# A decode-attention kernel with ScalarE's steady state as a loop, TensorE's loop two tiles longer, and the first output projection in two column tiles

## Chip, cores, metric

The kernel runs on one core of one Trainium2 chip. The metric is device time of one execution, in microseconds (us); lower is better. Engines are named as in the profile: PE is TensorE's matmuls and PEld its weight loads, DVE is VectorE, ACT is ScalarE, POOL is GpSimd, and SP is SyncE, which here only issues DMA. A name with "q" at its end (SPq) is that engine's sequencer.

## The reference

Two independent attention blocks A and B, each with batch 8, one query position, 32 heads of 128, and a cache of 4096 positions, all in bf16; their results are concatenated.

```python
q = (x @ wq).reshape(B, 1, 32, 128).transpose(0, 2, 1, 3)      # x: [8, 1, 1024]
scores = einsum("bhqd,bhkd->bhqk", q, k_cache) * 128 ** -0.5   # k_cache: [8, 32, 4096, 128]
p = softmax(scores)
o = einsum("bhqk,bhkd->bhqd", p, v_cache)
out = o.transpose(0, 2, 1, 3).reshape(B, 1, 4096) @ wo
```

Every element of the caches is read once, so the kernel has to bring 1107 MB into SBUF.

## The kernel before

The work is cut into 64 tiles (`NQ`), one for each block, group of eight heads, and batch. A tile is 8 MB of K and 8 MB of V. Three SBUF slots (`ring`) hold K and V tiles in turn. The order on the DMA queue is wq A, K0, wq B, K1, V0, K2, V1, K3, and so on. SP issues the load of a tile when the last reader of the slot's previous tenant has finished.

```python
plan = [("wq", 0, 1), ("k", 0, 0), ("wq", 1, 2)]          # kind, number, slot
for n in range(NQ - 1):
    plan.append(("k", n + 1, (n + 1) % 2))
    plan.append(("v", n, 2))                              # every V but the last goes to slot 2
```

For each K tile, DVE multiplies by the broadcast query and folds once, in four chunks (`NR = 4`); PE sums the rest; DVE finishes the scores; ACT takes the exponential; PE multiplies with V. The query vectors come from two projections. Each is transposed by PE into PSUM (`misc`), and DVE copies it to SBUF (`qT`). The second projection and its four copies stand inside tile 0:

```python
def make_qT(c):
    for hb in range(HB):
        ...                                               # PE transposes eight heads into misc
        opQT[c] = opQT["last"] = add("dve", lambda e, hb=hb: e.tensor_copy(
            qT[:, c, hb * HQ * B:(hb + 1) * HQ * B], misc_bf16[:, 0:HQ * B]), [op])   # contiguous

for n in range(NQ):
    for r in range(NR):
        make_mul(s); make_red(s - 1); ...; fold = make_fold(s)
        if n == 0 and r == 1:
            make_q(1); make_qT(1)                         # waits for wq B
        if r == 2 and n >= 1: make_pv(n - 1, 0, RG // 2)
        if r == 3 and n >= 1: make_pv(n - 1, RG // 2, RG); make_acc(n - 1)
        if r == 2 and n + 1 < NQ: make_stage(n + 1); make_qbc(n + 1)
        make_eacc(s, fold); load_tiles(); ...
```

PE and DVE run tiles 3 to 62 as a loop of two tiles each; ACT's code is written out for all 64 tiles. At the end come the two output projections, each 128 matmuls of 256 columns in four column tiles of the array. The last weights arrive in three pieces, of 24, 6 and 2 rows (`wo_cuts`).

Of the kernel before, what the change touches and what calls it, by code (L numbers as in the profile page):

```python
# [13 lines left out]
class _Op:  # L14
    __slots__ = ("eng", "emit", "deps", "dma_key", "token", "sig")

    def __init__(self, eng, emit, deps, dma_key=None):
        self.eng = eng
        self.emit = emit
        self.deps = [d for d in deps if d is not None]  # L20
        self.dma_key = dma_key
        self.token = None
        self.sig = False
# [7 lines left out]
class _Program:  # L31
# [11 lines left out]
    def add(self, eng, emit, deps=(), dma_key=None):  # L43
        op = _Op(eng, emit, list(deps), dma_key)
        if dma_key is not None:
            self.counts[dma_key] = self.counts.get(dma_key, 0) + 16
            op.token = (dma_key, self.counts[dma_key])
        for d in op.deps:
            if not (d.eng == "pe" and eng == "pe"):
                d.sig = True  # L50
        self.ops[eng].append(op)
        return op
# [13 lines left out]
    def _waits(self, engname):  # L66
        waited, out = {}, []
        for op in self.ops[engname]:
            need = {}
            for d in op.deps:  # L70
                if d.eng == "pe" and engname == "pe":
                    continue
                key, val = d.token
                if need.get(key, 0) < val:
                    need[key] = val
            left = []
            for key, val in need.items():
                if waited.get(key, 0) < val:
                    waited[key] = val
                    left.append((key, val))  # L80
            out.append(left)
        return out

    def run(self, engname, eng, sems, loop=None):
        ops, waits = self.ops[engname], self._waits(engname)

        def emit(op):
            ins = op.emit(eng)
            if op.dma_key is not None:
                ins.then_inc(sems[op.dma_key], 16)  # L90
            elif op.sig:
                ins.then_inc(sems[op.eng], 1)

        def straight(lo, hi):
            for op, left in zip(ops[lo:hi], waits[lo:hi]):
                for key, val in left:
                    eng.wait_ge(sems[key], val)
                emit(op)
# [8 lines left out]
        step = {}  # L107
        for j in range(size):
            rows = [waits[lo + j] for lo in at[:-1]]
            for i, row in enumerate(rows):  # L110
                assert [k for k, _ in row] == [k for k, _ in rows[0]], (engname, j, i, rows[0], row)
                assert ops[at[i] + j].sig == ops[at[0] + j].sig
                for (key, val), (_, base) in zip(row, rows[0]):
                    if i:
                        assert (val - base) % i == 0 and step.setdefault(key, (val - base) // i) * i == val - base, (engname, j, key)
        straight(0, at[0])
        with eng.Fori(0, rounds) as i:
            grown = {s: eng.snap(i * s) for s in sorted(set(step.values()))}
            for j in range(size):
                for key, val in waits[at[0] + j]:  # L120
                    eng.wait_ge(sems[key], grown[step[key]] + val)  # L121
                emit(ops[at[0] + j])
        straight(at[-1], len(ops))


LOOPS = {"pe": True, "dve": True}


def _build_kernel(nc, caches, out):
# [21 lines left out]
    with es:  # L151
# [22 lines left out]
        o_sb = sb("o_sb", [128, NC, B * H], FP32)  # L174
        rl = sb("rl", [128, B], FP32)
        on_sb = sb("on_sb", [128, NC, H, B], BF16)
        orow = sb("orow", [128, DT], BF16)
# [44 lines left out]
        opOc, opNorm, opProj, opUse, opPM = {}, {}, {}, {}, {}  # L222
# [15 lines left out]

        def tile_of(kind, n):
            return ring[:, slot[(kind, n)], :]  # L240

        def load_tiles():
            while issued[0] < len(plan):
# [6 lines left out]
                if kind in ("k", "v"):  # L250
                    blk, b = divmod(n, B)
                    c, hb = divmod(blk, HB)
# [28 lines left out]
        def make_qT(c):  # L281
            for hb in range(HB):
                rows = slice(32 * hb, 32 * hb + B)

                def emit(e, rows=rows):
# [6 lines left out]
                    qT[:, c, hb * HQ * B:(hb + 1) * HQ * B], misc_bf16[:, 0:HQ * B]), [op])  # L292

        def make_stage(n):
            blk, b = divmod(n, B)
            c, hb = divmod(blk, HB)
            from_ = qT[:, c, :].rearrange("p (h b) -> p h b", b=B)[:, hb * HQ:(hb + 1) * HQ, b]
            opSt[n] = add("act", lambda e: e.activation(qst[:, n % 2, :].rearrange("p (j m) -> p j m", m=MP),  # L298
                                                        from_.unsqueeze(2).to_broadcast([128, HQ, MP]), ACTF.Copy),
                          [opQT[c], _at(opQb, n - 2)])  # L300
# [22 lines left out]
        def make_eacc(s, fold):  # L323
# [9 lines left out]
            opEacc[s] = add("pe", emit, [fold, c_ident, _at(opRed, s - 2)])  # L333
# [10 lines left out]
        def make_shift(n):  # L344
# [6 lines left out]
            opExp[n] = add("act", lambda e: e.activation(pe[:], s_sb[:, n % 2, :], ACTF.Exp, bias=ngm[:, n % 2:n % 2 + 1], scale=scale,  # L351
                                                         accum_out=rsum[:, n:n + 1]),
                           [opNgm[n], _at(opPM, n - 1)])
# [24 lines left out]
        def make_ext(n):  # L378
            blk, b = divmod(n, B)
            c, hb = divmod(blk, HB)  # L380
# [10 lines left out]
            opOc[n] = add("act", lambda e: e.activation(o_sb[MB * hb:MB * (hb + 1), c, H * b:H * (b + 1)], to, ACTF.Copy), [opExt[n]])  # L391


        def make_norm(c):
            ns = range(c * HB * B, (c + 1) * HB * B)

            def emit(e):
                for hb in range(HB):
                    x = e.matmul(misc[MB * hb:MB * (hb + 1), 0:B], own_m[:].rearrange("p j u -> p (j u)"),
                                 rsum[:, (c * HB + hb) * B:(c * HB + hb + 1) * B], start=True, stop=True, tile_position=(0, MB * hb))  # L400
# [4 lines left out]
                on_sb[:, c].rearrange("p r b -> p b r"), o_sb[:, c, :].rearrange("p (b r) -> p b r", b=B),  # L405
                rl[:].unsqueeze(2).to_broadcast([128, B, H]), ALU.mult), [rec, opOc[ns[-1]]])

        def make_proj(c):
            w = tile_of("wo", c)
            for i, (r0, r1) in enumerate(wo_cuts if c == NC - 1 else ((0, H),)):  # L410
                def emit(e, r0=r0, r1=r1):
                    for r in range(r0, r1):
                        for q in range(NT):
                            col = r * D + q * DT
                            x = e.matmul(proj[32 * q:32 * q + B, 0:DT], on_sb[:, c, r, :], w[:, col:col + DT],  # L415
                                         start=(r == 0), stop=(r == H - 1), tile_position=(0, 32 * q))
                    return x
                opProj[c] = add("pe", emit, [opNorm[c], opT[("wo", c, i)], c_proj] + outs[:1])
            ev = add("dve", lambda e: e.tensor_copy(orow[0:96 + B, :], proj[0:96 + B, 0:DT]), [opProj[c]] + outs[1:])  # L419
            outs[:] = [ev]  # L420
            outs.extend(dma(out[:, 0, c * D + q * DT:c * D + (q + 1) * DT], orow[32 * q:32 * q + B, :], ("out", 0), [ev],
                            "sp" if q % 2 == 0 else "act") for q in range(NT))
# [67 lines left out]
        loop = (3, 2, (NQ - 4) // 2)  # L490
# [6 lines left out]
        @block.tensor  # L497
        def _(eng):
            P.run("pe", eng, sems, loop if LOOPS["pe"] else None)

        @block.scalar
        def _(eng):
            P.run("act", eng, sems)

        @block.vector
        def _(eng):
            P.run("dve", eng, sems, loop if LOOPS["dve"] else None)
# [39 lines left out]
```

## Time and profile before

| | before |
|---|---|
| time, median of 3 runs | 2566.49 us (2566.16 to 2568.4) |
| span of the profiled run | 2565.5 us |
| DMA engines | 99.8% of 16 engines' span, mean 432 GB/s |
| busy: DVE, PE, ACT | 85%, 43%, 5% |

From the page of the kernel before: the DMA row of the 40 slices of the span (9 means 90% or more busy), GB/s in the same slices, and the queues (packets, MB, share of 16 engines).

```profile
DMA  9999999999999999999999999999999999999998
GB/s 425 426 437 431 435 431 435 431 436 431 435 435 432 435 431 436 430 437 430 437 431 435 431 434 432 434 433 433 433 433 432 434 433 433 433 434 432 434 432 379
...
q1 hardware_dynamic: 19360, 1107.32, 99.8%
q8 instruction: 9, 0.15, 0.0%
q10 hardware_dynamic: 96, 0.05, 0.0%
q14 instruction: 5, 0.04, 0.0%
```

There is no slack in the DMA engines. Each packet of 64 KB takes 2.42 us in nearly every case, so an engine runs at a pace of its own, and a tile of 8 MB lands every 19.35 us. The two "instruction" queues, 0.19 MB here, are the engines' program code.

The end, in the chain of waits of the kernel before (start, duration, what):

```profile
2521.07 36.21 DMA ring<-in_B_wo_dram
2557.29 0.14 issue
2557.43 5.35 PE proj L415 x117
2562.78 0.02 issue
2562.80 0.42 DVE orow L419
```

The first piece of the last weights lands at 2557.29 us, the projection takes 5.35 us, the copy 0.42 us, and the output's DMA carries the span to 2565.5 us.

### The profile page before, as it was taken

Reading aid. Unit: us, or ns where it says so; the run is one execution under the profiler, and the core shown is the slowest. Engines: PE = TensorE matmul, PEld = TensorE weight load, DVE = VectorE, ACT = ScalarE, POOL = GpSimd, SP = SyncE. Lnnn points to the kernel's source line nnn. Section 1 sums busy time; section 2 is a strip of 40 time slices with the busy share of each in tenths; the row PEclk is TensorE's granted clock in tenths of the full one; section 3 lists DMA queues with packets and bytes.
Section 4 is the critical chain, followed back from the end, with each engine's and each line's share of the span. In section 5 each row is a group of like instructions: output and inputs, shape, how many; then the busy total and the mean of one; then the engine's idle time right before and its main releaser. Section 6 shows DMA issues by size and latency. Waiting matters only on the chain.

```text
span 2565.5 us, 18370 instructions
## 1 busy us (share of the span) xinstructions
PE 1106.8 (43%) x7712; PEld 393.2 (15%) x7712; DVE 2170.7 (85%) x1043; ACT 129.9 (5%) x401; POOL 2.5 (0%) x14
## 2 busy tenths in 40 slices
PE   2543443443444444444443434444434434434434
PEld 0111111111111111111111111111111111111112
DVE  2898898898898898898888888988988988988983
ACT  1100000000000000000000000000000000000000
POOL 0000000000000000000000000000000000000000
PEclk7676676766766766766767767667766767667667
DMA  9999999999999999999999999999999999999998
GB/s 425 426 437 431 435 431 435 431 436 431 435 435 432 435 431 436 430 437 430 437 431 435 431 434 432 434 433 433 433 433 432 434 433 433 433 434 432 434 432 379
DMA packets 19470, 1107.56 MB, mean 432 GB/s; under 512 B 2224, under 2 KB 2288, under 8 KB 2432
## 3 DMA queue, kind: packets, MB, share of 16 engines
q1 hardware_dynamic: 19360, 1107.32, 99.8%
q8 instruction: 9, 0.15, 0.0%
q10 hardware_dynamic: 96, 0.05, 0.0%
q14 instruction: 5, 0.04, 0.0%
HBM read 1107.33 MB, written 0.03 MB: 432 GB/s over the span
## 4 chain that ended last, share of the span: by engine, by line
DMA 51%; DVE 28%; issue 16%; PE 4%; another core or an unknown queue 0%; ACT 0%; DVEq 0%; SPq 0%
DMA ring<-in_B_k_cache_dram 25%; DMA ring<-in_A_k_cache_dram 25%; DVE ring L316 10%; DVE ring L321 10%; PE red L331 4%; DVE s_sb L339 4%; DVE PM L356 3%; DMA ring<-in_B_wo_dram 1%; DVE rmax L345 1%; DVE rtmp L346 0%; PE proj L415 0%; ACT PM L277 0%; PE o L271 0%; DVEq L121 0%
## 5 line engine op out<-in xcount | busy, mean ns | idle before, releaser
L316 DVE TENSOR_TENSOR ring<-ring,qbc 128x8192 bf16<-128x8192 bf16 x256 | 1132.0, 4422 | 305.5 <-DMA ring<-in_B_k_cache_dram 153.9
L331 PE MATMUL red<-ring,ident 128*128 128x512 bf16 x2048 | 775.6, 548 | 1396.5 <-DVE ring L321 1396.5
L321 DVE TENSOR_TENSOR ring<-ring 128x4096 bf16<-128x4096 bf16 x256 | 582.6, 2276 | 0.0
L331 PEld LDWEIGHTS red<-ring,ident 128*128 128x128 bf16 x2048 | 237.7, 127 | 1843.6 <-DVE ring L321 1498.7
L339 DVE TENSOR_REDUCE s_sb<-red 128x64 f32<-128x1024 f32 x256 | 312.2, 1220 | 2.5 <-PE red L331 2.5
L368 PE MATMUL pv<-ring,PM 128*32 128x512 bf16 x4096 | 269.5, 410 | 4.6 <-DVE PM L356 4.6
L356 DVE TENSOR_TENSOR PM<-pe,own_h 128x2048 bf16<-128x2048 bf16 x64 | 146.2, 2285 | 0.7 <-ACT pe L351 0.7
L368 PEld LDWEIGHTS pv<-ring,PM 128*32 128x32 bf16 x4096 | 103.2, 103 | 182.8 <-issue 108.0
L305 ACT ACTIVATE qbc<-misc 128x128 bf16<-128x128 f32 x64 | 17.7, 277 | 1070.0 <-PE misc L303 1070.0
L351 ACT ACTIVATE pe<-s_sb,ngm 128x256 bf16<-128x256 f32 x64 | 32.5, 508 | 477.3 <-DVE ngm L349 477.3
L376 ACT ACTIVATE accS<-pv 128x512 bf16<-128x512 f32 x64 | 38.2, 597 | 356.3 <-PE pv L368 356.3
L386 PEld LDWEIGHTS o<-accS,E 128*32 128x32 bf16 x1024 | 31.4, 101 | 49.8 <-issue 48.6
L386 PE MATMUL o<-accS,E 128*32 128x32 bf16 x1024 | 38.1, 185 | 0.7 <-ACT accS L376 0.7
L391 ACT ACTIVATE o_sb<-o 32x32 f32<-32x32 f32 x64 | 11.8, 185 | 440.5 <-PE o L386 439.8
L291 DVE COPY qT<-misc 128x64 bf16<-128x64 bf16 x8 | 1.5, 192 | 33.1 <-PE misc L287 33.1
L345 DVE TENSOR_REDUCE rmax<-s_sb 128x1 f32<-128x256 f32 x64 | 26.9, 420 | 2.2
L419 DVE CAST orow<-proj 104x256 bf16<-104x256 f32 x2 | 0.8, 425 | 27.6 <-PE proj L415 27.6
L415 PE MATMUL proj<-ring,on_sb 128*8 128x256 bf16 x256 | 11.1, 357 | 18.5 <-DMA ring<-in_A_wo_dram 9.6
L298 ACT ACTIVATE qst<-qT 128x128 bf16<-128x128 bf16 x64 | 18.7, 293 | 1.0 <-DVE qT L291 1.0
L346 DVE TENSOR_SCALAR rtmp<-half,rmax 128x32 f32<-128x32 f32 x64 | 15.5, 242 | 2.2
L271 PE MATMUL o<-ring,xT 128*8 128x512 bf16 x64 | 7.0, 615 | 20.0 <-DMA ring<-in_A_wq_dram 11.0
L349 DVE TRANSPOSE_TENSOR_REDUCE ngm<-rtmp 128x1 f32<-128x32 f32 x64 | 13.5, 211 | 2.2
(33 smaller groups left out, 74.9 us busy)
## 6 DMA issues: line engine op xcount, KB each, us to landing
ring<-in_B_wo_dram SPq DMA_DIRECT2D x1, 6144.0 KB, 36.2
ring<-in_B_wo_dram SPq DMA_DIRECT2D x1, 1536.0 KB, 39.5
ring<-in_A_k_cache_dram SPq DMA_DIRECT2D x32, 40.0
ring<-in_A_v_cache_dram SPq DMA_DIRECT2D x32, 27.9
ring<-in_B_k_cache_dram SPq DMA_DIRECT2D x32, 39.8
ring<-in_B_v_cache_dram SPq DMA_DIRECT2D x32, 27.9
ring<-in_B_wo_dram SPq DMA_DIRECT2D x1, 512.0 KB, 40.3
out_dram<-orow SPq DMA_DIRECT2D x4, 4.0 KB
```

The costliest lines, as they stand in the source:

```text
L298: opSt[n] = add("act", lambda e: e.activation(qst[:, n % 2, :].rearrange("p (j m) -> p j m", m=MP), from_.unsqueeze(2).to_broadcast([128, ...
L305: opQbc[n] = add("act", lambda e: e.activation(qbc[:, n % 2, :], misc[:, 0:Dh], ACTF.Copy), [opQb[n], _at(opMul, NR * (n - 2) + NR - 1)])
L316: opMul[s] = add("dve", lambda e: e.tensor_tensor(v, v, qbc[:, n % 2, :].unsqueeze(1).to_broadcast([128, CT, Dh]), ALU.mult), [opT[("k", n ...
L321: return add("dve", lambda e: e.tensor_tensor(v[:, :, 0:64], v[:, :, 0:64], v[:, :, 64:128], ALU.add), [opMul[s]])
L331: i = e.matmul(dst, ident[:], v[:, g, :, j, :], start=(j == 0), stop=(j == 3))
L339: opRed[s] = add("dve", lambda e: e.tensor_reduce(s_sb[:, n % 2, r * CT:(r + 1) * CT], red_ps[s % 2][:, :].rearrange("p (t w) -> p t w", w ...
L345: m = add("dve", lambda e: e.tensor_reduce(rmax[:], s_sb[:, n % 2, :], AX.X, ALU.max), [opRed[NR * n + NR - 1]])
L351: opExp[n] = add("act", lambda e: e.activation(pe[:], s_sb[:, n % 2, :], ACTF.Exp, bias=ngm[:, n % 2:n % 2 + 1], scale=scale, accum_out=rs ...
L356: opPM[n] = add("dve", lambda e: e.tensor_tensor(PM[:], pe[:].unsqueeze(2).to_broadcast([128, T, HQ]), own_h[:].unsqueeze(1).to_broadcast( ...
L368: i = e.matmul(pv_ps[32 * q:32 * (q + 1), :], PM[:, t:t + 4, :].rearrange("p t j -> p (t j)"), v[:, t * Dh:(t + 4) * Dh], start=(g == 0), ...
L376: opAcc[n] = add("act", lambda e: e.activation(accS[:], pv_ps[:], ACTF.Copy), [opPV[n], _at(opExt, n - 1)])
L386: x = e.matmul(to, E[:, i, PH - 1 - u:PH - 1 - u + MB], accS[:, i * 128 + H * u:i * 128 + H * (u + 1)], start=(i == 0 and u == 0), stop=(i ...
```

## The change

The intent is to make the program shorter: ACT's 60 steady tiles become a loop of four tiles, PE's loop starts at tile 1 instead of 3, and the first output projection becomes 64 matmuls of 512 columns. The program builds ACT's loop on addresses that move by a constant each round, so tiles are now visited with batch outside the head group, `o_sb` is flattened, and `qT` is stored batch by batch. The core of the diff (the bookkeeping of waits against loop counters is cut):

```diff
-                    blk, b = divmod(n, B)
-                    c, hb = divmod(blk, HB)
+                    c, b, hb = where(n)              # n // (B * HB), n // HB % B, n % HB
...
                 opQT[c] = opQT["last"] = add("dve", lambda e, hb=hb: e.tensor_copy(
-                    qT[:, c, hb * HQ * B:(hb + 1) * HQ * B], misc_bf16[:, 0:HQ * B]), [op])
+                    qT[:, c].rearrange("p (b h) -> p h b", h=H)[:, hb * HQ:(hb + 1) * HQ, :],
+                    misc_bf16[:, 0:HQ * B].rearrange("p (j b) -> p j b", b=B)), [op])
...
-        from_ = qT[:, c, :].rearrange("p (h b) -> p h b", b=B)[:, hb * HQ:(hb + 1) * HQ, b]
+            def emit(e, at):
+                from_ = qT[:].rearrange("p c n -> p (c n)")[:, bass.ds(at(n * HQ, HQ), HQ)]
...
-            opEacc[s] = add("pe", emit, [fold, c_ident, _at(opRed, s - 2)])
+            opEacc[s] = add("pe", emit, [fold, c_E, _at(opRed, s - 2)])
...
+            nt = NT if c == NC - 1 else NT // 2
+            dt = D // nt
...
-        loop = (3, 2, (NQ - 4) // 2)
+        loops = {"pe": (1, 2, (NQ - 2) // 2), "dve": (3, 2, (NQ - 4) // 2), "act": (3, HB, (NQ - 4) // HB)}
```

More of the change, by code (lines that the diff above doesn't have):

```diff
@@ L14, with __init__ @@
 class _Op:
-    __slots__ = ("eng", "emit", "deps", "dma_key", "token", "sig")
-    def __init__(self, eng, emit, deps, dma_key=None):
+    __slots__ = ("eng", "emit", "deps", "dma_key", "token", "sig", "moves")
+    def __init__(self, eng, emit, deps, dma_key=None, moves=False):
         self.eng = eng
         self.emit = emit
+        self.moves = moves
         self.deps = [d for d in deps if d is not None]
@@ L41, in __init__, with add @@
         self.marks = {}
-    def add(self, eng, emit, deps=(), dma_key=None):
-        op = _Op(eng, emit, list(deps), dma_key)
+    def add(self, eng, emit, deps=(), dma_key=None, moves=False):
+        op = _Op(eng, emit, list(deps), dma_key, moves)
         if dma_key is not None:
@@ L66, in _waits @@
     def _waits(self, engname):
-        waited, out = {}, []
+        waited, out, known = {}, [], []
         for op in self.ops[engname]:
@@ L75, in _waits, with emit @@
                     need[key] = val
-            left = []
+            left = {}
             for key, val in need.items():
                 if waited.get(key, 0) < val:
-                    waited[key] = val
-                    left.append((key, val))
+                    left[key] = val
             out.append(left)
-        return out
+            known.append(dict(waited))
+            waited.update(left)
+        return out, known
     def run(self, engname, eng, sems, loop=None):
-        ops, waits = self.ops[engname], self._waits(engname)
-        def emit(op):
-            ins = op.emit(eng)
+        ops = self.ops[engname]
+        waits, known = self._waits(engname)
+        def emit(op, at=lambda base, step: base):
+            ins = op.emit(eng, at) if op.moves else op.emit(eng)
             if op.dma_key is not None:
@@ L95, in straight @@
             for op, left in zip(ops[lo:hi], waits[lo:hi]):
-                for key, val in left:
+                for key, val in left.items():
                     eng.wait_ge(sems[key], val)
@@ L106, in run, with place @@
         assert all(y - x == size for x, y in zip(at, at[1:]))
-        step = {}
+        body, step = [], {}
         for j in range(size):
             rows = [waits[lo + j] for lo in at[:-1]]
-            for i, row in enumerate(rows):
-                assert [k for k, _ in row] == [k for k, _ in rows[0]], (engname, j, i, rows[0], row)
+            row = {}
+            for key in rows[1]:
+                grow = rows[2][key] - rows[1][key]
+                row[key] = rows[1][key] - grow
+                assert step.setdefault(key, grow) == grow
+                assert rows[0].get(key) == row[key] or key not in rows[0] and row[key] <= known[at[0] + j].get(key, 0), (engname, j, key)
+            for i, r in enumerate(rows):
                 assert ops[at[i] + j].sig == ops[at[0] + j].sig
-                for (key, val), (_, base) in zip(row, rows[0]):
-                    if i:
-                        assert (val - base) % i == 0 and step.setdefault(key, (val - base) // i) * i == val - base, (engname, j, key)
+                assert set(r) <= set(row) and (i == 0 or r == {key: val + i * step[key] for key, val in row.items()}), (engname, j, i)
+            body.append(row)
         straight(0, at[0])
         with eng.Fori(0, rounds) as i:
-            grown = {s: eng.snap(i * s) for s in sorted(set(step.values()))}
+            grown = {x: eng.snap(i * x) for x in sorted(set(step.values()))}
+            moved = {}
+            def place(base, x):
+                if x not in moved:
+                    moved[x] = eng.snap(i * (x * per))
+                return moved[x] + base
             for j in range(size):
-                for key, val in waits[at[0] + j]:
+                for key, val in body[j].items():
                     eng.wait_ge(sems[key], grown[step[key]] + val)
-                emit(ops[at[0] + j])
+                emit(ops[at[0] + j], place)
         straight(at[-1], len(ops))
-LOOPS = {"pe": True, "dve": True}
 def _build_kernel(nc, caches, out):
@@ L173, in _build_kernel @@
         accS = sb("accS", [128, 512], BF16)
-        o_sb = sb("o_sb", [128, NC, B * H], FP32)
+        o_sb = sb("o_sb", [128, NC * B * H], FP32)
         rl = sb("rl", [128, B], FP32)
         on_sb = sb("on_sb", [128, NC, H, B], BF16)
-        orow = sb("orow", [128, DT], BF16)
+        orow = sb("orow", [128, 2 * DT], BF16)
         q_sb = PM[:].rearrange("p t j -> p (t j)").rearrange("p (c n) -> p c n", c=NC)
@@ L221, in _build_kernel @@
         opPV, opAcc, opExt, opSt, opQb, opQbc, opQ, opQs, opQT = {}, {}, {}, {}, {}, {}, {}, {}, {}
-        opOc, opNorm, opProj, opUse, opPM = {}, {}, {}, {}, {}
+        opOc, opNorm, opProj, opUse, opPM, opEv = {}, {}, {}, {}, {}, {}
         outs = []
@@ L237, in _build_kernel, with where @@
         issued = [0]
+        def where(n):
+            return n // (B * HB), n // HB % B, n % HB
         def tile_of(kind, n):
@@ L291, in make_qT @@
                 opQT[c] = opQT["last"] = add("dve", lambda e, hb=hb: e.tensor_copy(
-                    qT[:, c, hb * HQ * B:(hb + 1) * HQ * B], misc_bf16[:, 0:HQ * B]), [op])
+                    qT[:, c].rearrange("p (b h) -> p h b", h=H)[:, hb * HQ:(hb + 1) * HQ, :],
+                    misc_bf16[:, 0:HQ * B].rearrange("p (j b) -> p j b", b=B)), [op])
         def make_stage(n):
-            blk, b = divmod(n, B)
-            c, hb = divmod(blk, HB)
-            from_ = qT[:, c, :].rearrange("p (h b) -> p h b", b=B)[:, hb * HQ:(hb + 1) * HQ, b]
-            opSt[n] = add("act", lambda e: e.activation(qst[:, n % 2, :].rearrange("p (j m) -> p j m", m=MP),
-                                                        from_.unsqueeze(2).to_broadcast([128, HQ, MP]), ACTF.Copy),
-                          [opQT[c], _at(opQb, n - 2)])
+            def emit(e, at):
+                from_ = qT[:].rearrange("p c n -> p (c n)")[:, bass.ds(at(n * HQ, HQ), HQ)]
+                return e.activation(qst[:, n % 2, :].rearrange("p (j m) -> p j m", m=MP),
+                                    from_.unsqueeze(2).to_broadcast([128, HQ, MP]), ACTF.Copy)
+            opSt[n] = add("act", emit, [opQT[n // (B * HB)], _at(opQb, n - 2)], moves=True)
         def make_qbc(n):
@@ L350, in make_shift @@
                                                             apply_transpose=True), [t, _at(opExp, n - 2)])
-            opExp[n] = add("act", lambda e: e.activation(pe[:], s_sb[:, n % 2, :], ACTF.Exp, bias=ngm[:, n % 2:n % 2 + 1], scale=scale,
-                                                         accum_out=rsum[:, n:n + 1]),
-                           [opNgm[n], _at(opPM, n - 1)])
+            opExp[n] = add("act", lambda e, at: e.activation(pe[:], s_sb[:, n % 2, :], ACTF.Exp, bias=ngm[:, n % 2:n % 2 + 1], scale=scale,
+                                                             accum_out=rsum[:, bass.ds(at(n, 1), 1)]),
+                           [opNgm[n], _at(opPM, n - 1)], moves=True)
         def make_pm(n):
@@ L378, in make_ext @@
         def make_ext(n):
-            blk, b = divmod(n, B)
-            c, hb = divmod(blk, HB)
+            hb = where(n)[2]
             to = o_ps[0:MB, H * (n % 2):H * (n % 2 + 1)]
@@ L390, in make_ext @@
             opExt[n] = add("pe", emit, [opAcc[n], c_E, _at(opOc, n - 1)] + (list(opQs.values()) if n == 0 else []))
-            opOc[n] = add("act", lambda e: e.activation(o_sb[MB * hb:MB * (hb + 1), c, H * b:H * (b + 1)], to, ACTF.Copy), [opExt[n]])
+            opOc[n] = add("act", lambda e, at: e.activation(o_sb[MB * hb:MB * (hb + 1), bass.ds(at(n // HB * H, H // HB), H)], to, ACTF.Copy),
+                          [opExt[n]], moves=True)
         def make_norm(c):
@@ L399, in emit @@
                     x = e.matmul(misc[MB * hb:MB * (hb + 1), 0:B], own_m[:].rearrange("p j u -> p (j u)"),
-                                 rsum[:, (c * HB + hb) * B:(c * HB + hb + 1) * B], start=True, stop=True, tile_position=(0, MB * hb))
+                                 rsum[:].rearrange("p (n h) -> p h n", h=HB)[:, hb, c * B:(c + 1) * B], start=True, stop=True, tile_position=(0, MB * hb))
                 return x
@@ L404, in make_norm @@
             opNorm[c] = add("dve", lambda e: e.tensor_tensor(
-                on_sb[:, c].rearrange("p r b -> p b r"), o_sb[:, c, :].rearrange("p (b r) -> p b r", b=B),
+                on_sb[:, c].rearrange("p r b -> p b r"), o_sb[:, c * B * H:(c + 1) * B * H].rearrange("p (b r) -> p b r", b=B),
                 rl[:].unsqueeze(2).to_broadcast([128, B, H]), ALU.mult), [rec, opOc[ns[-1]]])
@@ L412, in emit @@
                     for r in range(r0, r1):
-                        for q in range(NT):
-                            col = r * D + q * DT
-                            x = e.matmul(proj[32 * q:32 * q + B, 0:DT], on_sb[:, c, r, :], w[:, col:col + DT],
+                        for q in range(nt):
+                            col = r * D + q * dt
+                            x = e.matmul(proj[32 * q:32 * q + B, 0:dt], on_sb[:, c, r, :], w[:, col:col + dt],
                                          start=(r == 0), stop=(r == H - 1), tile_position=(0, 32 * q))
                     return x
-                opProj[c] = add("pe", emit, [opNorm[c], opT[("wo", c, i)], c_proj] + outs[:1])
-            ev = add("dve", lambda e: e.tensor_copy(orow[0:96 + B, :], proj[0:96 + B, 0:DT]), [opProj[c]] + outs[1:])
-            outs[:] = [ev]
-            outs.extend(dma(out[:, 0, c * D + q * DT:c * D + (q + 1) * DT], orow[32 * q:32 * q + B, :], ("out", 0), [ev],
-                            "sp" if q % 2 == 0 else "act") for q in range(NT))
+                opProj[c] = add("pe", emit, [opNorm[c], opT[("wo", c, i)], c_proj, opEv.get(c - 1)])
+            rows = 32 * (nt - 1) + B
+            opEv[c] = add("dve", lambda e: e.tensor_copy(orow[0:rows, 0:dt], proj[0:rows, 0:dt]), [opProj[c]] + outs)
+            for q in range(nt):
+                outs.append(dma(out[:, 0, c * D + q * dt:c * D + (q + 1) * dt], orow[32 * q:32 * q + B, 0:dt],
+                                ("out", 0), [opEv[c]], "sp" if q % 2 == 0 else "act"))
         x_sb = ring[0:B, 2, 0:NC * D].rearrange("p (c d) -> p c d", c=NC)
@@ L498, in _ @@
         def _(eng):
-            P.run("pe", eng, sems, loop if LOOPS["pe"] else None)
+            P.run("pe", eng, sems, loops["pe"])
         @block.scalar
         def _(eng):
-            P.run("act", eng, sems)
+            P.run("act", eng, sems, loops["act"])
         @block.vector
         def _(eng):
-            P.run("dve", eng, sems, loop if LOOPS["dve"] else None)
+            P.run("dve", eng, sems, loops["dve"])
         @block.gpsimd
```

## The prediction

> **What bounds the kernel now.** The DMA engines. The page's DMA row is 9 in nearly every slice at 431 to 437 GB/s, and the input queue's packets fill 99.8% of 16 engines' span. A 64 KB packet takes 2.42 us (median), so each engine runs at its own fixed pace, 27.1 GB/s, and tile after tile of 8 MB lands every 19.35 us. [...] Compute is not in the way: VectorE is 85% busy and needs about 34 us of each 38.7 us tile pair; ScalarE is 5% busy, TensorE 43%. In steady state V loads are issued 28 us and K loads 40 us before they land (list of DMA issues), 8 to 20 us ahead of need.
>
> **What the change does.** Bytes and steady-state work stay; tiles are visited with batch outside the head block, so that ScalarE's body repeats every four tiles with register-computed addresses. ScalarE gets register operations (32 to 63 ns each in VectorE's loop), a few per tile: not critical. 60 tiles of ScalarE code and two of TensorE code become loop rounds. The new order cannot help packets that already run at a fixed pace.
>
> The first output projection goes from 128 matmuls of 256 in four column tiles (5.83 us) to 64 of 512 in two. A group of matmuls at 512 columns takes 0.427 us at half clock and about 0.216 at full (from the trace), so 32 groups take 9 to 14 us (estimate). It starts near 2542.7 us and the last weights it precedes land at 2557.3: hidden, narrowly at worst.
>
> **What can reach the critical path: instruction fetches.** They share the 16 DMA engines. The landings of one transfer's 16 parts spread over 0.45 us at the start but 4.46 us at the end: one engine is 2.7 us behind the next slowest. Its lag grows by about 1.2 us after a 16 KB fetch at 36.5 us, 0.65 after fetches at 223 and 230, and 0.7 after each of the 8 KB fetches at 1055 and 1876 us. The last two (and 1473, on another engine) fit ScalarE's straight code, 64 recorded instructions apart. The end hangs on the slowest engine: first piece of the last weights lands 2557.29, projection 5.35, copy 0.42, output write to 2565.5 (chain of waits). A ScalarE loop removes the late fetches, up to 1.4 us on that engine, but adds one or two at loop entry and first back edge, as VectorE's loop shows near 155 and 230 us. [...] Net estimate: 0.7 to 1.4 us less, the tail's clock phase moving it by half a microsecond either way.
>
> **Prediction.** 2565.4 us, 8 in 10 between 2563.0 and 2567.6. Faster by over 2%: 0.5%; within 2%: 99%; slower by over 2%: 0.5%.
>
> **What would show it.** No 8 KB fetches after about 400 us; last transfer's spread near 3 to 3.8 us rather than 4.46; steady pace still 19.35 us per tile; first projection 9 to 14 us, ending before the second's weights land; V issues still 28 us ahead.
>
> **What would make it wrong.** A ScalarE loop body that [...] is fetched again each round: 15 rounds at 0.7 us on one or two engines, 5 to 20 us more. TensorE's tail fetches falling on the slowest engine. Dynamic addresses costing several us per tile.

The 5 to 20 us of the last paragraph are the estimate from the steps of 0.7 us. That fetches take time of the engines that move the data is read from the landings in the trace of the kernel before: across the fetch at 1055.48 us one of a transfer's 16 parts, the slowest, fell back by 0.68 us against the first, and no other moved by more than 0.02; across the fetch at 1473.56 us a part that had landed within 0.32 us of the first came to land 0.81 us after it, and the slowest kept its 3.6. Of the register operations, the 32 ns are PE's shortest in that trace; DVE's took 40 to 63.

## More of the kernel before

The start, in the timeline of the kernel before (start, duration, engine, line, operation, and in brackets the idle time before it and what ended it):

```profile
69.58 0.19 DVE L291 COPY qT<-misc 128x64 bf16<-128x64 bf16 x1 [11.88 <-PE misc L287]
70.29 0.19 DVE L291 COPY qT<-misc 128x64 bf16<-128x64 bf16 x1 [0.52 <-PE misc L287]
71.00 0.19 DVE L291 COPY qT<-misc 128x64 bf16<-128x64 bf16 x1 [0.52 <-PE misc L287]
71.72 0.19 DVE L291 COPY qT<-misc 128x64 bf16<-128x64 bf16 x1 [0.52 <-PE misc L287]
71.83 4.42 DVE L316 TENSOR_TENSOR ring<-ring,qbc 128x8192 bf16<-128x8192 bf16 x1
...
117.25 0.33 SPq L198 DMA_DIRECT2D ring<-in_A_v_cache_dram  x1
...
160.28 4.43 DVE L316 TENSOR_TENSOR ring<-ring,qbc 128x8192 bf16<-128x8192 bf16 x1 [5.38 <-DMA ring<-in_A_k_cache_dram]
```

DVE stands still from 57.7 to 69.6 us, because the copies of the second projection stand before its next multiply. From 71.8 to 154.9 us it never waits. So until then DVE sets the pace, and through PE it sets when SP may issue the V load at 117.25 us.

## The result, and the profile after

The changed kernel took 2566.69 us (median of 4 runs, 2566.15 to 2567.29) and the kernel before 2566.6 us in the same rounds (4 runs, 2566.16 to 2568.4). The ratio is 0.9999, with a 95% interval of 0.9982 to 1.0016: the same. Ratios here are the mean time of one kernel's fast runs over the mean of the other's of the same rounds, so not quite the ratio of the medians quoted.

From the page of the changed kernel, the same rows:

```profile
DMA  9999999999999999999999999999999999999998
GB/s 425 425 425 441 433 433 433 433 435 431 435 431 435 431 435 432 435 431 435 432 435 431 435 431 436 430 436 430 437 429 437 429 437 430 436 431 435 431 436 381
...
q1 hardware_dynamic: 19344, 1107.32, 99.8%
q8 instruction: 7, 0.11, 0.0%
q10 hardware_dynamic: 80, 0.05, 0.0%
q14 instruction: 4, 0.02, 0.0%
```

The fetches are fewer, as intended: nine packets became seven on one queue, all of 16 KB, and five of 8 KB became three on the other (its fourth packet has 96 bytes). The start, in the timeline of the changed kernel:

```profile
69.66 0.43 DVE L305 COPY qT<-misc 128x64 bf16<-128x64 bf16 x1 [11.99 <-PE misc L301]
70.61 0.43 DVE L305 COPY qT<-misc 128x64 bf16<-128x64 bf16 x1 [0.52 <-PE misc L301]
71.57 0.43 DVE L305 COPY qT<-misc 128x64 bf16<-128x64 bf16 x1 [0.52 <-PE misc L301]
72.52 0.44 DVE L305 COPY qT<-misc 128x64 bf16<-128x64 bf16 x1 [0.52 <-PE misc L301]
72.67 4.54 DVE L330 TENSOR_TENSOR ring<-ring,qbc 128x8192 bf16<-128x8192 bf16 x1
...
118.20 0.33 SPq L209 DMA_DIRECT2D ring<-in_A_v_cache_dram  x1
...
161.99 4.42 DVE L330 TENSOR_TENSOR ring<-ring,qbc 128x8192 bf16<-128x8192 bf16 x1 [6.14 <-DMA ring<-in_A_k_cache_dram]
```

Here is something that the prediction had not priced. The copies to `qT` take 0.43 us instead of 0.19, so DVE's next multiply starts 0.84 us later, the V load is issued 0.95 us later, and the K tile that DVE waits for at 160 us is there 1.71 us later. The windows view of both kernels has the time around 118 us (columns: window, its length, busy time and count of PE, PEld, DVE, ACT, POOL, granted clock, DMA share, GB/s). Before:

```profile
117.00:122.00 5.00, 1.07 (x7) 0.33 (x4) 5.00 (x4) 0.60 (x1) 0.00 (x0) 0.83 0.99 406
122.00:140.00 18.00, 7.25 (x32) 2.39 (x31) 17.90 (x11) 0.99 (x4) 0.00 (x0) 0.59 0.96 412
```

After:

```profile
117.00:122.00 5.00, 1.16 (x24) 0.34 (x16) 5.00 (x4) 0.60 (x1) 0.00 (x0) 0.85 0.68 236
122.00:140.00 18.00, 7.73 (x32) 2.57 (x32) 17.90 (x11) 0.99 (x4) 0.00 (x0) 0.59 1.07 460
```

At first sight the DMA engines moved 236 GB/s in these five microseconds instead of 406. But the view counts a packet in the window in which it starts, and the second packets of the new tile start just before 122 us in the kernel before and mostly just after it in the changed one. The next window makes up for it (460 against 412), and the two windows together have 411 GB/s in both kernels. So this view does not show the loss; the trace's packet records do. In the kernel before, most of the new tile's first packets start between 118.7 and 119.0 us, just as the old tile's last ones end: over the 16 engines the mean gap is 0.09 us. In the changed kernel they start at 119.16 us or later, 0.96 us after the issue, and the mean gap is 0.61 us: the queue had run dry. The first packets are slow as well, with a median of 3.11 us, against 2.67 in the kernel before and 2.42 for a packet inside a transfer.

The end, in the chain of waits of the changed kernel:

```profile
2521.87 34.98 DMA ring<-in_B_wo_dram
2556.84 0.14 issue
2556.98 5.66 PE proj L433 x96
2562.64 0.02 issue
2562.66 0.42 DVE orow L438
```

Against the kernel before, the first piece of the last weights lands 0.45 us earlier, and the projection then takes 0.31 us longer, so the copy starts 0.14 us earlier. The span is 0.2 us shorter.

One further reading of the trace is used below. A transfer is spread over 16 DMA engines, and the trace records when each finished its part. "First part" is the fastest engine's, "last part" the slowest's, and their distance is the "spread". For the last piece of the last weights:

| | V1 issued | first part of V1 | last weights: first part | last part | spread |
|---|---|---|---|---|---|
| before | 117.25 | 138.51 | 2557.73 | 2562.18 | 4.45 |
| after | 118.20 | 139.50 | 2558.53 | 2561.74 | 3.21 |

So two things happened in this pair of traces. All engines were late by about 0.8 us at the end, and the slowest engine was 1.24 us less behind the fastest. They leave 0.44 us. The first comes from the dry queue. Is the second the effect of ACT's loop, as predicted? The experiments ask both. One thing can be read from these two traces already: in the changed kernel the spread went from 1.66 us on K2 to 2.99 on V1, because one engine began V1 only at 121.84 us, when the other 15 had begun by 120.24. All the rest of the run, with the fetches that the loop leaves, added 0.2 us. In the kernel before it went from 1.83 to 2.28 us on V1 and grew to 4.45 later.

### The profile page after: what moved, and what is told of

It reads as the page before. It is cut to its first block, busy times and chain, and to the rows that moved or that the text cites. A ratio compares the mean times of both kernels' runs of the same rounds, so it can differ in the third digit from the quotient of the medians.

```text
span 2565.3 us, 18707 instructions
## 1 busy us (share of the span) xinstructions
PE 1125.5 (44%) x7648; PEld 395.3 (15%) x7648; DVE 2172.4 (85%) x1043; ACT 130.0 (5%) x401; POOL 2.6 (0%) x14
## 4 chain that ended last, share of the span: by engine, by line
DMA 51%; DVE 28%; issue 16%; PE 5%; another core or an unknown queue 0%; ACT 0%; DVEq 0%; SPq 0%
DMA ring<-in_B_k_cache_dram 25%; DMA ring<-in_A_k_cache_dram 25%; DVE ring L330 10%; DVE ring L335 10%; PE red L345 4%; DVE s_sb L353 4%; DVE PM L370 3%; DMA ring<-in_B_wo_dram 1%; DVE rmax L359 1%; DVE rtmp L360 0%; PE proj L433 0%; ACT PM L291 0%; PE o L285 0%; DVEq L135 0%
## 5 line engine op out<-in xcount | busy, mean ns | idle before, releaser
L345 PE MATMUL red<-ring,ident 128*128 128x512 bf16 x2048 | 785.6, 553 | 1380.5 <-DVE ring L335 1380.5
L405 ACT ACTIVATE o_sb<-o 32x32 f32 (+1 forms) x64 | 11.9, 186 | 454.4 <-PE o L399 453.8
L433 PE MATMUL proj<-ring,on_sb 128*8 128x256 bf16 (+1 forms) x192 | 15.2, 395 | 13.8 <-DMA ring<-in_A_wo_dram 8.7
L312 ACT ACTIVATE qst<-qT 128x128 bf16 (+1 forms) x64 | 18.7, 293 | 2.0 <-DVE qT L305 2.0
## 6 DMA issues: line engine op xcount, KB each, us to landing
ring<-in_A_v_cache_dram SPq DMA_DIRECT2D x32, 27.9
ring<-in_B_v_cache_dram SPq DMA_DIRECT2D x32, 27.9
```

The lines of the kernel that those rows point to most:

```text
L312: return e.activation(qst[:, n % 2, :].rearrange("p (j m) -> p j m", m=MP), from_.unsqueeze(2).to_broadcast([128, HQ, MP]), ACTF.Copy)
L345: i = e.matmul(dst, ident[:], v[:, g, :, j, :], start=(j == 0), stop=(j == 3))
```

## The experiments

Theory A: the strided copies delay DVE, the V1 load is then issued when the queue is all but empty, and the shift stays to the end. In addition ACT's straight code costs the slowest engine 1.4 us in late fetches. Rivals: B, TensorE's loop entry at tile 1 delays V1; C, the smaller spread has nothing to do with ACT's loop. Times are compared as the mean of a kernel's five runs minus the mean of the kernel before on the same chip. One kernel's runs scatter with a standard deviation of 0.2 to 1.4 us, so the traces carry most of the argument. No ratio's interval leaves 2% either side.

**e1: the copies made short again, all else kept.**

```diff
-        qT = sb("qT", [128, NC, H * B], BF16)
+        qT = sb("qT", [128, H * NC * B], BF16)
-                    qT[:, c].rearrange("p (b h) -> p h b", h=H)[:, hb * HQ:(hb + 1) * HQ, :],
+                    qT[:].rearrange("p (h n) -> p h n", h=H)[:, hb * HQ:(hb + 1) * HQ, c * B:(c + 1) * B],
```

(ACT's read of `qT` and its step per loop round were adapted to this layout.)

> The changed kernel with qT laid out (head, batch) so that each copy out of PSUM writes runs of 8 contiguous elements; everything else kept. Theory A (the strided qT copies, 0.43 us each against 0.19 before, hold VectorE up by 0.85 us at 72 us, so the V load that is issued at 118.2 us instead of 117.25 finds the DMA queue nearly empty, and the shift stays to the end): copies back near 0.2 us, that issue at 117.3 to 117.5, the first part of the seventh transfer lands near 138.6 instead of 139.5, last weights land near 2560.9 instead of 2561.7, span about 0.8 us under the changed kernel's 2565.3. Rival B (TensorE's loop entry at tile 1 delays it): issue stays at 118.2 and the last weights at 2561.7.

From the groups of instructions of e1 (busy us, mean ns):

```profile
L305 DVE COPY qT<-misc 128x64 bf16<-128x64 bf16 x8 | 1.5, 192 | 33.4 <-PE misc L301 33.4
```

V1 was issued at 117.44 us and its first part landed at 138.78. Both are as Theory A has them and not as B. The end was a miss: the last weights landed at 2562.09 us, not 2560.9. Up to the transfer before them the spread was 2.65 us, and on the last it was 4.2; a 16 KB fetch of program code ran at 2547.8 us. Times: 2565.39 us median, mean 0.26 us under the kernel before; three runs were at 2564.8 to 2565.4, two at 2567.4 and 2567.8. The profiled run is one of these last two.

**e2: the kernel before with the strided copies alone** (the same two lines, `qT` stored as "b h" in each block, with ACT's read adapted).

> The kernel before with the changed kernel's strided qT copies alone. Theory A: copies 0.43 us, the V load issued at 118.2 us instead of 117.25, last weights land near 2563.1 instead of 2562.2, span 0.8 to 1 us over the kernel before. Rival B: copies slower, but the issue at 117.3 to 117.5 and the end as before.

V1 was issued at 118.37 us, its first part landed at 139.89, and the mean time was 0.92 us over the kernel before (2567.27 us median, 2566.8 to 2567.73). The copies alone delay V1 and shift the transfer, without ACT's loop or PE's longer one. The profiled end is again a miss: the last weights landed at 2562.11 us and not 2563.1, because the spread was 2.93 us, not 4.45. Yet ACT's code is straight here, with 8 KB fetches at 1057, 1475 and 1876 us.

**e3: the changed kernel with ACT's loop undone.**

```diff
-            P.run("act", eng, sems, loops["act"])
+            P.run("act", eng, sems)
```

> The changed kernel with ScalarE's code straight again (no loop). Theory A with fetches on the slowest engine: 8 KB fetches return near 1055, 1475 and 1876 us, two of them 0.7 us each on the slowest engine, spread of the last transfer's parts 4.2 to 4.7 us instead of 3.2, last weights near 2563 us, span 1 to 1.4 us over the changed kernel. Rival C (the smaller spread of the changed kernel has nothing to do with ScalarE's loop): spread stays at 3.0 to 3.4 and the end as changed.

The fetches were there, at 1056.5, 1474.6 and 1877.2 us (the changed kernel has one at 1474.7 us too), and the spread was 2.82 us: smaller than the changed kernel's, not larger. The last weights landed at 2561.46. The median was 2566.88 us, mean 0.40 over the kernel before. The second half of Theory A fails: in this trace the slowest engine's lag did not step at any of the three. Rival C fits, though its range for the spread was missed by 0.2 us.

**e4: the changed kernel with PE's loop from tile 3 again.**

```diff
-        loops = {"pe": (1, 2, (NQ - 2) // 2), ...
+        loops = {"pe": (3, 2, (NQ - 4) // 2), ...
```

> The changed kernel with TensorE's loop from tile 3 again. Theory A: V load still issued at 118.2 us; one or two more 16 KB fetches between 180 and 230 us; end within 0.7 us of the changed kernel. Rival B: V load issued at 117.3, seventh transfer at 138.6, last weights near 2560.9, span 0.8 us less.

V1 was issued at 118.51 us, so B falls: PE's loop entry did not delay it. 16 KB fetches at 185.7 and 222.0 us came back. The last weights landed at 2560.81 us (spread 1.84), 0.93 us before the changed kernel's and outside the 0.7 us allowed, but the last projection took 6.27 us on PE instead of 5.63, and the mean time was 0.79 us over the kernel before. A single trace's end is no measure of such a change.

**r_before and r_after: both kernels once more, unchanged,** to see what of a trace repeats.

> The kernel before once more, unchanged, for its trace. Theory A': instruction fetches fall on engines that vary from run to run: fetch times as in the first trace within 2 us, V load issued at 117.3 +- 0.3, first part of the seventh transfer 138.4 to 138.9, but the late fetches need not fall on the slowest engine: spread of the last transfer anywhere in 2.2 to 4.7 us. Theory A (the fetches' engines are fixed by the program): spread 4.3 to 4.6 us again, last weights 2562.1 +- 0.3.

> The changed kernel once more, unchanged, for its trace. V load issued at 118.2 +- 0.3, first part of the seventh transfer 139.3 to 139.9 under either theory. Spread 3.2 +- 0.2 and last weights 2561.7 +- 0.3 if the program fixes which engine serves a fetch; spread anywhere in 1.9 to 4.0 if it varies.

| | V1 issued | first part of V1 | last weights: last part | spread |
|---|---|---|---|---|
| before, first trace | 117.25 | 138.51 | 2562.18 | 4.45 |
| before, again | 117.55 | 139.00 | 2561.62 | 3.46 |
| after, first trace | 118.20 | 139.50 | 2561.74 | 3.21 |
| after, again | 118.43 | 139.59 | 2561.74 | 3.08 |

The start repeats within 0.3 us in time of issue and within 0.5 us in the first part of V1. The spread of the kernel before does not: with fetches again at 1056.2, 1474.0 and 1876.9 us, the slowest engine's lag did not step at any of them, while in the first trace it stepped by 0.7 us at two. Whether a fetch meets the slowest engine is not fixed by the program. The records do not name the engine, so they do not tell whether the fetch falls on another engine or another engine is the slowest.

**e6: a dose.** Eight more strided copies on DVE at 70 us, into a tile not yet in use; the result is right.

```diff
+                for i in range(2 * c):
+                    add("dve", lambda e, at=2 * hb + i: e.tensor_copy(
+                        accS[:].rearrange("p (b h) -> p h b", b=B)[:, at * HQ:(at + 1) * HQ, :],
+                        misc_bf16[:, 0:HQ * B].rearrange("p (j b) -> p j b", b=B)), [op])
```

> The changed kernel with eight more strided copies of 0.4 us on VectorE at 70 us (into a tile not in use yet; result unchanged). Theory A: the V load at 118.2 us is issued 3.2 to 3.6 us later, at about 121.6, and as the queue is dry by then every later landing shifts by as much: first part of the seventh transfer near 143, last weights near 2565, span 3 us over the changed kernel. If the queue had slack there: less than 1 us.

The eight copies cost less than assumed: V1 was issued at 120.50 us, 2.30 later than in the changed kernel. Its first part landed at 141.73, later by 2.23: one for one. The median was 2568.74 us, mean 2.59 over the kernel before. The last weights' last part was at 2562.74 us, only 1.0 us later than in the changed kernel (2565 was expected), while the first part was 2.17 later (2560.70). The same difference stands at V1 already: its last part landed 1.05 us later (143.54 against 142.49), since no engine fell behind the others here as one did in the changed kernel. All 16 first packets of V1 ended within 0.57 us of each other, though the engines had ended K2 1.72 us apart, so in a dry spell of this length those that were behind caught up. (By the end of V1, with two fetches in between, the spread was 1.81 us again.)

**e7: the second query projection moved from tile 0's second chunk to its last,** strided copies kept.

```diff
-                if n == 0 and r == 1:
+                if n == 0 and r == 3:
                     for c in range(1, NC):
                         make_q(c)
                         make_qT(c)
```

> The changed kernel with the second query projection moved from tile 0's second chunk to its last one, so VectorE does not stand still from 57 to 70 us waiting for the second wq; strided copies kept. Theory A (the lasting shift is the queue running dry at 118 us): the third V/K-pair's V load is issued between 108 and 114 us instead of 118.2, the first part of the seventh transfer lands at 138.3 to 138.6 instead of 139.5, and the shift of 1 us is absent to the end: last weights land at 2559.2 to 2561.0 (a late instruction fetch on the slowest engine would give the upper figure), span 2562.5 to 2564.5. If the strided copies cost in another way than by the dry queue, nothing is won.

DVE's 12 us wait for wq B is gone, K2's load moves from 91.9 to 80.8 us, and V1's to 112.30. From the timeline of e7:

```profile
80.78 0.33 SPq L209 DMA_DIRECT2D ring<-in_A_k_cache_dram  x1
112.30 0.33 SPq L209 DMA_DIRECT2D ring<-in_A_v_cache_dram  x1
```

The first part of V1 landed at 138.30 us, exactly 19.35 after the transfer before it. Its first packets start 0.01 us after the old ones end and take 2.42 us: no dry spell. The last weights landed at 2559.45, 2.3 us before the changed kernel's. All five runs (2564.16 to 2565.08, median 2564.61) lie below all nine of the kernel before on that chip (2565.12 to 2566.67); the difference of the means is 1.41 us. The strided copies are still there and cost nothing now. All expected numbers held.

**e10: the same move in the kernel before** (the same edit).

> The kernel before with the second query projection moved from tile 0's second chunk to its last. Theory D (the queue's dry moment at 118 us is the one thing that moved the end; a V load must be issued some 1.9 us before the queue drains, and the kernel before stood on that edge): V load issued near 112 us, first part of the seventh transfer 138.3, last weights 2559.2 to 2561.0, span 2562.5 to 2564.5: as e7, within 0.7 us, without anything of the change. Rival E (the gain of e7 needed the loops): span as the kernel before, 2564.5 to 2565.5.

V1 was issued at 112.22 us, its first part landed at 138.44, the last weights at 2559.74. The span of the profiled run was 2563.7 us; the mean was 1.76 us under the kernel before (median 2565.41). The gain needs nothing of the change. It is more than V1's first part was late in the kernel before (0.1 or 0.7 us). The traces show the rest on the slowest engine: the spread at the end was 2.03 us here, against 4.45 and 3.46. How much of that comes from the dry moment (on V1 the spread is 1.74 us here, against 2.28 and 2.96) and how much from the draw of the fetches is not separated.

**e9: e7 with ACT's code straight** (the edit of e3).

> The kernel of e7 with ScalarE's code straight. If ScalarE's fetches matter only by the engine they happen to fall on: 8 KB fetches return near 1056, 1474 and 1877 us, the mean landing of the last weights is 0.1 to 0.2 us later than in e7 (three fetches of 0.7 us over 16 engines), the median of the runs 0 to 0.7 us over e7's. If they always cost: 1.4 us over e7's.

The fetches were at 1053.0, 1471.2 and 1873.7 us (e7 has only the middle one), and the last weights landed at 2559.52 us, against 2559.45 in e7. The mean over the 16 parts was 2558.46 against 2558.41 (0.05 later; 0.1 to 0.2 was expected). The median, 2565.56 us, is 0.95 over e7's, more than the 0.7 allowed, but e7 ran on another chip. In the traces the copy after the last projection starts 0.87 us later than in e7, though the weights landed within 0.07 us: PE needed 6.07 us for that projection here. Against the kernel before on the same chip the two gain the same: 1.49 and 1.41 us. So ACT's loop is worth less than these runs resolve.

**e5: the changed kernel with the first output projection in four column tiles.**

```diff
-            nt = NT if c == NC - 1 else NT // 2
+            nt = NT
```

> The changed kernel with the first output projection in four column tiles of 256 again. It is done before the second's weights land either way: first projection 5.5 to 6.9 us instead of 9.5, last weights 2561.7 +- 0.4, median within 0.7 us of the changed kernel. If the two-tile form cost or won anything on the critical path, over 1 us of difference.

The first projection took 5.77 us instead of 9.54, and ended at 2548.1 us, long before the second's weights came at 2556.84 in both. The last weights landed at 2561.75 us, against 2561.74. The median was 2566.42 us. The two-tile form is off the critical path. V1 was issued at 118.90 us here, 0.7 later than in the changed kernel, though nothing was changed at the start, so that the last parts agree so well is partly luck. Over the runs with strided copies in the old place (e6 left out) the issue lies between 118.05 and 118.90 us, over those with short copies between 117.25 and 117.55.

**e8: e7, with e1's short copies and the last weights in four pieces.**

```diff
-        wo_cuts = ((0, H - 8), (H - 8, H - 2), (H - 2, H))
+        wo_cuts = ((0, H - 16), (H - 16, H - 6), (H - 6, H - 2), (H - 2, H))
```

> e7 with the short qT copies of e1 and the last weights in four pieces of 16, 10, 4 and 2 rows instead of 24, 6 and 2. Last weights land as in e7 (2559.2 to 2561), but TensorE starts the last projection some 5 us earlier and has only the last two rows left then, so the end follows the last landing by 3.3 us instead of 3.5 to 3.8; median 0 to 0.5 us under e7's. If TensorE was not behind there: the same as e7.

The timeline of e8 at its end shows that PE now works through the weights as they come:

```profile
2550.74 1.92 PE L434 MATMUL proj<-ring,on_sb 128*8 128x256 bf16 x64 [0.78 <-DVE orow L439]
...
2556.31 2.31 PE L434 MATMUL proj<-ring,on_sb 128*8 128x256 bf16 x40 [3.65 <-DMA ring<-in_B_wo_dram]
...
2558.79 1.03 PE L434 MATMUL proj<-ring,on_sb 128*8 128x256 bf16 x16 [0.17 <-DMA ring<-in_B_wo_dram]
...
2559.99 0.60 PE L434 MATMUL proj<-ring,on_sb 128*8 128x256 bf16 x8 [0.18 <-DMA ring<-in_B_wo_dram]
...
2560.64 0.42 DVE L439 CAST orow<-proj 104x256 bf16<-104x256 f32 x1 [9.96 <-PE proj L434]
```

The median was 2564.51 us, mean 2.43 us under the kernel before. All five runs (2564.31 to 2565.03) lie below all nine of that kernel on the same chip (2565.85 to 2568.39), and below e9's five (2565.21 to 2565.7). The end follows the last landing by 3.35 us (3.3 was expected; 3.43 in e7). It is the largest gain of the runs, but of three edits at once, and not divided among them; the ratio, 0.9990 (0.9977 to 1.0004), is still "the same" by a 2% measure. In its trace all engines lost 0.45 us at K1, at 80 us, for a reason not found, and the last weights landed at 2559.95 us, so this look does not show its best.

## Why the prediction was right or wrong

**Right: the bound.** The DMA engines set the time, and the pace was 19.35 us per tile in all 14 traces after the start. The mean was 432 GB/s in the kernel before and in the changed one. The tile order, ACT's register-computed addresses and the register operations cost nothing that is seen (ratio of the times 0.9999), and the loops' code was not fetched again each round: the span of the changed kernel's trace has ten fetches in all. V loads were still issued 27.9 us before landing.

**Right: the first output projection.** It took 9.54 us (9 to 14 predicted) and was hidden; e5 shows that it plays no part.

**Right in the trace, but not by the cause given: the spread.** The prediction asked for 3 to 3.8 us and the changed kernel had 3.21. But e3, with the fetches back, had 2.82, and the kernel before, run again, had 3.46 with the same fetches. In the changed kernel 2.99 us of it were there on V1 already, before any of the fetches that the loop removes. The failed step is this one, as the prediction put it: "A ScalarE loop removes the late fetches, up to 1.4 us on that engine". The late fetches at 1055 and 1876 us did go; a fetch near 1474 us stayed in every variant, so it was never ACT's straight code, as the prediction had it. What failed was to read a property of the program from one trace. The two steps of 0.7 us on the slowest engine were there in the first trace of the kernel before; the slowest engine did not step so in that kernel's second trace, in e2 or in e3. Spread over 16 engines, two fetches of 0.7 us are worth about 0.1 us (estimate); e9 against e7 measured 0.05.

**Missing: the copies to `qT`.** "Bytes and steady-state work stay" was true, and the prediction then looked at the steady state and the end alone. Four copies at 70 us grew from 0.19 to 0.43 us. The runs show which form is slow: with 64 contiguous elements, in the kernel before, a copy took 0.192 us; with runs of eight contiguous elements, in e1, 0.192 us again; with a stride of 32 elements, 0.435. Why the stride costs 0.24 us was not shown. Four copies, each 0.24 us longer, make 0.96 us, and the V1 load was 0.95 later.

**Why so early a delay reached the end.** DVE sets the pace until 155 us, and V1's issue stood on an edge. In the ten traces with the projection in its old place, V1's first part lands 21.2 to 21.5 us after its issue, whenever that was (117.25 to 120.50). In e7, e9 and e10, where it is issued at 112 us, it lands 19.35 us after the transfer before it, at 138.3 to 138.4. So the issue has to come about 2 us before the first part of K2 lands, at 119.0 us. The kernel before issued at 117.25 or 117.55 and lost 0.1 or 0.7 us against that; the changed one issued at 118.20 or 118.43 and lost 1.2 or 1.3. Later tiles are issued 8 to 20 us ahead and have such slack; this one had none. In a queue that is full from there on, what is lost is lost for good: e6 carries a dose to the first part one for one, and e7 and e10 win 1.4 and 1.8 us by moving the issue 5 to 6 us forward.

The packet and landing records give the same for all 16 engines instead of the fastest alone. "Gap" is the mean time between an engine's last packet of K2 and its first of V1; "late" is how much more than 19.35 us after K2 the 16 parts of V1 landed, on the mean.

| | V1 issued | gap | first packets, median | late | spread, K2 to V1 | last weights, mean of the parts |
|---|---|---|---|---|---|---|
| before | 117.25 | 0.09 | 2.67 | 0.37 | 1.83 to 2.28 | 2559.01 |
| before, again | 117.55 | 0.23 | 2.98 | 0.88 | 2.08 to 2.96 | 2559.42 |
| after | 118.20 | 0.61 | 3.11 | 1.33 | 1.66 to 2.99 | 2559.64 |
| after, again | 118.43 | 0.89 | 3.01 | 1.42 | 1.92 to 2.95 | 2559.77 |
| e6 | 120.50 | 2.67 | 3.14 | 3.37 | 1.77 to 1.81 | 2561.61 |
| e7 | 112.30 | 0.01 | 2.42 | 0.10 | 1.80 to 1.87 | 2558.41 |
| e10 | 112.22 | 0.01 | 2.42 | 0.10 | 1.71 to 1.74 | 2558.71 |

So the late issue costs in two ways, by the gap and by slow first packets, and in four of the five late rows the slowest engine falls further behind as well. What a run lost on V1 against e7 stands in the last weights again, within 0.45 us in all 13 traces that have these pieces (e8 has others).

**Net.** The forecast was 0.7 to 1.4 us less. In its place: 0.6 to 1.0 us more lost at 118 us than before (first parts of the two pairs of traces; the mean time of e2, with nothing else changed, is 0.92 us up), something like 0.1 us won by fewer fetches, and the draw of how often a fetch meets the slowest engine, up to 1.4 us in one trace. The means differ by 0.24 us (2566.70 against 2566.94), well inside the scatter of the runs. The 2566.69 us lie in the predicted range because it was wide enough for one term of this size that was not in the sum. To that extent it was luck: the forecast gain is not there, and in the first pair of traces the missing term (0.80 us) and the smaller spread (1.24 us) happened to pull against each other.

**The tail's clock phase** was given half a microsecond either way. The last projection took 5.32 us on PE before, 5.63 after, 6.27 in e4, 6.01 in e10: somewhat more. Over the first two of these stretches the granted clock was 0.68 and 0.64. e8's earlier pieces take most of it off the chain.

**Open.** Why a 16 KB fetch, at 785 us in the changed kernel, comes at a different time in each variant (315 us in e1, 394 in e3, 624 in e7) and even in the same kernel run again (243.8 us) was not followed. Nor was it found why in several runs with a late issue one engine begins V1 a microsecond or more after the others, or why the first packets are slow. That e1's late loss comes from the fetch at 2547.8 us is argued from its time and size, not shown, since the packet records used do not name the engine.

## What to carry to other kernels

In a kernel at the DMA bound, look for the moments when the queue holds little work; here an issue less than about 2 us before the first part of the load ahead landed was too late. There was one such moment, at the start, where a compute engine still set the pace, and about a microsecond on that engine (four copies of a quarter more each) counted in full. Later loads were issued 8 to 20 us ahead of need, so the same delay should cost nothing there (an estimate from that lead; no run tested it). A change that is "for the loop" also changes layouts, so price every instruction that reads or writes a tile whose layout moved, even if it runs eight times. And a step of under a microsecond on one DMA engine in one trace can be a draw (the steps of 0.7 us in one trace of the kernel before were not in the other): trace the same kernel twice before building a sum on it.
